# Turn-taking between VectorE and GpSimd in a fused GeGLU FFN (Strassen-Winograd) kernel

## The chip, the cores and the metric

One core of one Trainium2 chip. The metric is the device time of one launch in microseconds, median of several executions. In every execution here it is 1.7 to 1.9 us longer than the span of the profile (first to last instruction), and the granted TensorE clock was 0.998 to 1.000, so all runs are compared as fast ones. The runs came from several chips of the same kind; only kernels timed in the same rounds on the same chip are compared by ratio.

## The reference

```python
B, S, D, F = 1, 2048, 1024, 3584          # all bfloat16
def reference(x, w_gate, w_up, w_down):
    return (gelu_tanh(x @ w_gate) * (x @ w_up)) @ w_down
```

## The kernel before

The kernel computes each 2x2 block product with seven products in place of eight (Winograd's form). Sums of blocks of x (t1 to t4), of the gate and up weights (s1 to s4) and of w_down are made beside the matmuls. Rows are done in two halves (h = 0, 1); in each half the f tiles go in 14 pairs. In a pair TensorE does m1, m2 (of the pair before), m6, m5, m7, m3, m4, 8 matmuls each. Meanwhile GpSimd makes the 8 weight sums of the next pair, VectorE adds product m5 to banks in PSUM and multiplies by the gelu, and, in the first half only, VectorE makes 42 "staging" sums of w_down rows, into a pool of four buffers (o_sb) from which 28 of them are stored to DRAM for the later stage. A buffer of the same pool, the "x tile" below, is now and then filled with transposed x for the second half (DMA transposes) and stored to DRAM too. The parts that the change touches (cuts are marked):

```python
def pool(inst):
    if "pool_wait" in last_on:                       # a semaphore wait, once
        tc.add_manual_dep(inst.ins, last_on.pop("pool_wait").ins.name, SYNC_DEP, reason="port")
    return on("pool", inst)
def pool_behind_dve():
    last_on["pool_wait"] = last_on["dve"]
...                                                  # t_sum, for t4: all blocks on VectorE
    dve(tt(out=t[:, cs], in0=b(1, 0)[:, cs], in1=t2[:, cs], op=sub))
...                                                  # stage_step(n): one staging sum
    dve(nc.vector.tensor_tensor(out=t, in0=in0, in1=in1, op=ALU.subtract))
    if k > 0:
        sp(nc.sync.dma_start(out=t_dram[:, k - 1, i, :], in_=t.bitcast(F32)))
...                                                  # the loop over pairs, h == 0, pair >= 2
    n = [min(max(4 * (pair - PPG + d) - 2, 0), NSTEP) for d in range(3)]
    steps = [lambda k=k: stage_step(k) for k in range(n[0], n[1])]
    early_steps = steps[: len(steps) - 2]
    then["m2 of last"] = (load_chunk if any) + early_steps + (fill an x tile)
    then["m7"] = [load rows of w_down for the next pair] + [store_x]
    then["m4"] = steps[len(early_steps) :]           # two of them behind m4
```

So a pair's four staging sums stand in two places: two behind the last matmuls, in front of the next pair's product `out11` (the multiplication behind m2), two behind that. Nothing keeps them off GpSimd's sums.

Of the kernel before, what the change touches and what calls it, by code (L numbers as in the profile page):

```python
# [34 lines left out]
def kernel(  # L35
# [87 lines left out]
        return on("act", inst)  # L123

    def dve(inst):
        return on("dve", inst)

    def pool(inst):
        if "pool_wait" in last_on:

            tc.add_manual_dep(
                inst.ins, last_on.pop("pool_wait").ins.name, SYNC_DEP, reason="port"
            )
        return on("pool", inst)

    def pool_behind_dve():
        last_on["pool_wait"] = last_on["dve"]

    def pe(inst):
        return on("pe", inst)  # L140
# [86 lines left out]
    def t_sum(name, c0=0, c1=KH):  # L227
        def b(j, l):
            return xT[l][:, half(j), :]

        t0 = ("t1", "t2", "t3", "b22", "t4").index(name) * KH * TB
        t = t_mem[:, t0 : t0 + KH * TB].rearrange("p (a b) -> p a b", b=TB)
        tsum[name] = t
        sub = ALU.subtract
        tt = nc.vector.tensor_tensor
        if name == "t1":
            dve(tt(out=t, in0=b(0, 1), in1=b(0, 0), op=sub))
        elif name == "t2":
            t1 = tsum["t1"].bitcast(F32)
            dve(tt(out=t, in0=b(1, 1), in1=t1, op=sub))  # L240
        elif name == "t3":
            dve(tt(out=t, in0=b(1, 1), in1=b(0, 1), op=sub))
        elif name == "t4":
            t2 = tsum["t2"].bitcast(F32)
            cs = slice(c0, c1)
            dve(tt(out=t[:, cs], in0=b(1, 0)[:, cs], in1=t2[:, cs], op=sub))  # L246
        else:
            for c in range(KH):
                act(nc.scalar.copy(out=t[:, c, :], in_=b(1, 1)[:, c, :]))
# [126 lines left out]
    S_NAMES = ("s1", "s2", "s3", "s4", "a22")  # L376


    pending = []

    def pair_quads(hT, h, pair, nxt, then, part=None):
# [20 lines left out]
                f()  # L402

        def prep(j, name):
            if nxt is not None and part is None:
                s_sum(nxt[0], nxt[1], j, name)

        def s(j, name):
# [26 lines left out]
        def do_m5(j):  # L435
            mm(V_[j], j, s(j, "s1"), tsum["t1"], True)
            m5[j] = m_pool.tile([P, TB], F32, name=f"m5_{j}")
            act(nc.scalar.copy(out=m5[j][:], in_=banks[V_[j]][:]))  # L438
            prep(j, "s1")

        def do_m6(j):
            mm(QB[j], j, s(j, "s2"), tsum["t2"], False)
# [30 lines left out]
        for j in range(2):  # L473
            add_m5(QB[j], QB[j])
            done(f"q{j}")
            prep(j, "s2")
        done("m5")
        for j in range(2):
# [111 lines left out]


    staged = {}
    NSTEP = 3 * NS

    def stage_load(i):
        w = wd_pool.tile([P, WDT, D], BF16, name="wd_sb")
# [5 lines left out]
    def stage_step(n):  # L602
# [11 lines left out]
        if k > 0:  # L614
            sp(nc.sync.dma_start(out=t_dram[:, k - 1, i, :], in_=t.bitcast(F32)))



    staged_x = []

    def stage_x(tb, kd):
        if tb == 1:
            load_xT(xT, 1, tb, kd, kd + 1)
            return
        t = o_pool.tile([P, 1, TB], BF16, name="o_sb")
        src = xv[SH : SH + TB, kd : kd + 1, :]
        sp(nc.sync.dma_start_transpose(out=t[:], in_=src))
        staged_x.append((x_dram[:, kd : kd + 1, :], t[:]))

    def store_x():  # L630
        for dst, src in staged_x:
# [197 lines left out]
    for h in range(NH):  # L829
        hT = hT_pool.tile([P, KF, SH], BF16, name="hT")  # L830
        first_pair = 0
        if h == 0:
            first_units(hT)
            first_pair = PPG - 1

            nxt = (0, PPG)
            for j in range(2):
                s_sum(0, first_pair, j, "s3")
            pair_quads(hT, 0, first_pair, nxt, {}, 0)
            t_sum("t1")  # L840
            for j in range(2):
                s_sum(0, first_pair, j, "a22")
                for name in ("s1", "s2"):
                    s_sum(0, first_pair, j, name, True)
            for k0, k1 in ((0, KH // 2), (KH // 2, KH), (KH, KD)):
                for u, bset in enumerate((PB, RB)):
                    for b, w_sb in zip(bset, chunks[first]):
                        for kd in range(k0, k1):
                            mm_gu(banks[b], w_sb, u, 1, kd)
                    if k1 == KD:  # L850
                        unit_out(hT, bset, u, 1)
                    if k1 == KD and u == 0:
                        t_sum("t3")
                if k1 == KH:
                    out11 = pair_quads(hT, 0, first_pair, nxt, {}, 2)
                    t_sum("b22")
                    t_sum("t2")
                    s_sum(0, first_pair, 0, "s4", True)
            t_sum("t4", 0, KH // 2)
            s_sum(0, first_pair, 1, "s4", True)  # L860

            xs = [
                (tb, kd + i) for kd in range(0, KD, 2) for tb in (1, 0) for i in range(2)
            ]
            new_x(1)
            stage_load(0)
        for pair in range(first_pair, NPAIR):
            then = {}
            if pair % PPG == 0 and (pair // PPG + 1) * PPG < NPAIR:
                key = (h, pair // PPG + 1)  # L870

                def load_chunk(key=key):
                    new_chunk(key)
                    for j in range(2):
                        load_w(key, j, 0, KD, act)

                if key not in chunks:
                    then["m2 of last"] = [load_chunk]
            if h == 0 and pair >= PPG:

                n = [
                    min(max(4 * (pair - PPG + d) - 2, 0), NSTEP) for d in range(3)
                ]
                steps = [lambda k=k: stage_step(k) for k in range(n[0], n[1])]
                early_steps = steps[: len(steps) - 2]
                new = range((n[1] + 2) // 3, (n[2] + 2) // 3)

                then["m2 of last"] = (
                    then.get("m2 of last", [])
                    + early_steps  # L890
                    + [lambda q=q: stage_x(*q) for q in xs[:2]]
                )
                then["m7"] = [lambda i=i: stage_load(i) for i in new] + [store_x]
                then["m4"] = steps[len(early_steps) :]
                xs = xs[2:]
            if pair == NPAIR - 2:

                then.setdefault("m2 of last", []).extend(
# [1 line left out]
                )  # L900
            if 6 < pair < 11:
                i = 2 * pair - 8
                then.setdefault("m6", []).append(
                    lambda i=i: s_down(hT, 0, "s3", i, i + 2)
                )
            if pair == NPAIR - 1:
                then |= {
                    "m2 of last": [
                        lambda: load_b22(4, 10),
                        lambda: load_b22(10, NS),  # L910
                        lambda: early.append(
                            wd_pool.tile([P, WDT, D], BF16, name="wd_sb")
                        ),
                        lambda: s_down(hT, 0, "s3", 0, 4),
                    ],
                    "m6": [
                        lambda: s_down(hT, 0, "s1", 4, 8),
                        lambda: t_down(0, "t1", 4, 6),
                    ],
                    "m2": [  # L920
                        lambda: load_wd_rows(8, 10),
                        lambda: load_wd_rows(10, 12),
                        lambda: load_wd_rows(12, NS),
                        lambda: load_b22(0, 4),
                    ],
                    "m7": [lambda: s_down(hT, 0, "s1", 0, 4)],
                    "m3": [lambda: t_down(0, "t1", 0, 2)],
                    "m4": [
                        lambda: t_down(0, "t2", 0, NT2),
                        lambda: t_down(0, "t1", 2, 4),  # L930
                        lambda: t_down(0, "t1", 6, 8),
                        lambda: s_down(hT, 0, "s1", 8, NS),
                        lambda: t_down(0, "t1", 8, NS),
                    ],
                }
            if pair < PPG and h == 0:

                def late_t4(c):
                    t_sum("t4", c, c + 1)
                    last_on["t4"] = last_on["dve"]  # L940

                def late_s():
                    last_on["pool_wait"] = last_on["t4"]
                    for name in S_NAMES:
                        for j in range(2):
                            s_sum(0, PPG, j, name)

                then = {
                    "q0": [lambda: late_t4(KH - 2)],
                    "v0": [lambda: late_t4(KH - 1)],  # L950
                    "v1": [out11],
                    "m4": [late_s],
                }
# [6 lines left out]
        if h + 1 < NH:  # L960
# [1 line left out]
            new_x(0)  # L962

            def x_fill():
                sp(nc.sync.dma_start(out=xT[0][:], in_=x_dram[:]))

            def w_fill(c, j):
                if j == 0:
                    new_chunk((nh, c))
                n = 2 if c == 0 else 1  # L970
                for k0 in range(0, KD, KD // n):
                    load_w((nh, c), j, k0, k0 + KD // n)

            def s_fill(j, *names):
                for name in names:
# [58 lines left out]
```

## Time and profile before

| | before |
|---|---|
| median of the 3 executions known at the time (lowest to highest) | 541.09 us (540.6 to 542.26) |
| the execution that was profiled: time, span | 542.15 us, 540.4 us |
| TensorE / VectorE / GpSimd busy | 99% / 67% / 43% |
| period of a pair in either half | 12.56 us |
| stalls of TensorE for VectorE | 1.37 us in pair 3, 0.40 us in pair 1 |

The groups of instructions by shape on VectorE between 40 and 176 us, for the line of the staging sums (count, then busy us and mean ns of one):

```profile
L613 DVE TENSOR_TENSOR o_sb<-wd_sb,o_sb 128x512 fp32r<-128x512 bf16 x28 | 29.9, 1066 | 0.5
...
L613 DVE TENSOR_TENSOR o_sb<-wd_sb 128x512 fp32r<-128x512 bf16 x14 | 18.6, 1328 | 0.0
```

A sum that takes 0.68 us when it is free takes 1.07 and 1.33 us on average here.

### The profile page before, as it was taken

To read this page: it belongs to the slowest core of one execution; us is meant where nothing else is said; L and a number is where in the kernel's file an instruction comes from. 1 tells how busy PE (TensorE), PEld (TensorE's weight loads), DVE (VectorE), ACT (ScalarE), POOL (GpSimd) and SP (SyncE) were. 2 spreads that over 40 slices of the span, in tenths; PEclk is the share of its full clock that TensorE was granted. 3 is DMA by queue.
4 is the path that set the end of the run, shared out by engine and by line. 5 is a ranking of instruction groups with operands and counts; after the bars stand their busy time and mean duration, and the time that the engine had idled before them with its cause. 6 is when DMAs were issued, how large, how long until landed. Compare 5 with 4: busy or idle time off the path is not lost.

```text
span 540.4 us, 7111 instructions
## 1 busy us (share of the span) xinstructions
PE 534.3 (99%) x2384; PEld 377.4 (70%) x2384; DVE 363.9 (67%) x478; ACT 263.4 (49%) x446; POOL 233.8 (43%) x208
## 2 busy tenths in 40 slices
PE   9999999999999999999999999999999999999997
PEld 4576777767676676767776667777777766866865
DVE  1968777787877997889474334444444469969951
ACT  2554555555555319217465555555555551552270
POOL 1078777777777000000056776666777730000000
PEclk9999999999999999999999999999999999999999
DMA  9952877795726968689950505041231466677855
GB/s 224 281 175 85 258 215 231 213 285 177 252 98 222 354 223 310 199 279 300 323 184 1 156 1 157 13 144 61 95 112 45 156 207 219 226 233 244 284 158 202
DMA packets 84372, 102.70 MB, mean 190 GB/s; under 512 B 18672, under 2 KB 66288, under 8 KB 84208
## 3 DMA queue, kind: packets, MB, share of 16 engines
q1 hardware_dynamic: 61936, 80.49, 46.1%
q10 hardware_dynamic: 22400, 21.76, 13.0%
q8 instruction: 19, 0.31, 0.2%
q14 instruction: 17, 0.14, 0.1%
HBM read 85.98 MB, written 12.58 MB: 182 GB/s over the span
## 4 chain that ended last, share of the span: by engine, by line
PE 97%; DVE 1%; DMA 1%; ACT 0%; issue 0%; ACTq 0%
PE bank L390 62%; PE bank L678 33%; PE bank L254 3%; DVE o_sb L613 1%; DMA w_mem<-in_x_dram 1%; PE bank L305 0%; DVE hT L278 0%; ACT s_mem L374 0%; ACT o_sb L731 0%; ACT w_mem L273 0%; DVE xT L313 0%; ACTq L731 0%; ACTq L374 0%
## 5 line engine op out<-in xcount | busy, mean ns | idle before, releaser
L390 PE MATMUL bank<-t_mem,s_mem 128*128 128x512 f32 x1056 | 250.0, 395 | 1.1 <-DVE hT L278 1.1
L390 PEld LDWEIGHTS bank<-t_mem,s_mem 128*128 128x128 f32 x1056 | 198.1, 188 | 45.7 <-DVE hT L278 1.5
L361 POOL TENSOR_TENSOR s_mem<-w_mem 128x512 fp32r<-128x512 bf16 x102 | 117.2, 1171 | 202.7 <-DVE t_mem L246 103.0
L678 PE MATMUL bank<-t_mem,s_mem 128*128 128x512 f32 x544 | 127.1, 392 | 0.0
L278 DVE TENSOR_TENSOR hT<-w_mem,bank 128x512 bf16<-128x512 f32 x104 | 71.0, 686 | 82.9 <-PE bank L390 42.9
L678 PEld LDWEIGHTS bank<-t_mem,s_mem 128*128 128x128 f32 x544 | 102.2, 188 | 22.1
L413 DVE TENSOR_TENSOR bank<-bank,m 128x512 f32<-128x512 f32 x108 | 69.9, 694 | 47.2 <-ACT m L438 43.9
L390 PE MATMUL bank<-xT,w_mem 128*128 128x512 bf16 x432 | 98.1, 380 | 0.0
L273 ACT ACTIVATE w_mem<-bank 128x512 f32<-128x512 f32 x104 | 61.8, 596 | 54.1 <-DVE bank L413 35.7
L390 PEld LDWEIGHTS <-w_mem 128*128 128x128 bf16 x432 | 40.2, 98 | 51.7 <-issue 6.8
L588 DVE TENSOR_TENSOR t_mem<-w_mem 128x1024 fp32r<-128x1024 bf16 x56 | 65.6, 1218 | 0.0
L361 POOL TENSOR_TENSOR s_mem<-w_mem,s_mem 128x512 fp32r<-128x512 bf16 x50 | 61.7, 1260 | 0.0
L361 POOL TENSOR_TENSOR s_mem<-s_mem,w_mem 128x512 fp32r<-128x512 f32 x50 | 57.6, 1173 | 0.0
L443 ACT COPY bank<-bank 128x512 f32<-128x512 f32 x54 | 30.8, 570 | 39.0 <-PE bank L390 38.5
L374 ACT CAST s_mem<-w_mem 128x512 fp32r<-128x512 bf16 x54 | 33.1, 616 | 31.9 <-PE bank L390 29.2
L438 ACT COPY m<-bank 128x512 f32<-128x512 f32 x54 | 31.7, 587 | 19.7 <-PE bank L390 19.2
L653 DVE TENSOR_TENSOR s_mem<-hT 128x512 fp32r<-128x512 bf16 x52 | 34.2, 686 | 10.1 <-PE bank L678 9.4
L678 PEld LDWEIGHTS <-hT 128*128 128x128 bf16 x224 | 21.3, 98 | 26.6 <-issue 2.1
L448 ACT COPY bank<-bank 128x512 f32<-128x512 f32 x54 | 30.7, 570 | 12.1 <-PE bank L390 12.1
L731 ACT CAST o_sb<-bank 128x512 bf16<-128x512 f32 x28 | 15.6, 586 | 39.2 <-PE bank L678 33.5
L613 DVE TENSOR_TENSOR o_sb<-wd_sb,o_sb 128x512 fp32r<-128x512 bf16 x28 | 29.9, 1066 | 0.5
L585 ACT CAST t_mem<-w_mem 128x1024 fp32r<-128x1024 bf16 x28 | 26.9, 1048 | 0.0
(45 smaller groups left out, 239.9 us busy)
## 6 DMA issues: line engine op xcount, KB each, us to landing
t_mem<-t_dram SPq DMA_DIRECT2D x56, 512.0 KB, 5.1
w_mem<-in_w_gate_dram ACTq DMA_DIRECT2D x10, 1024.0 KB, 5.7
w_mem<-in_w_up_dram ACTq DMA_DIRECT2D x10, 1024.0 KB, 7.9
wd_sb<-in_w_down_dram SPq DMA_DIRECT2D x28, 256.0 KB, 4.7
t_dram<-o_sb SPq DMA_DIRECT2D x28, 256.0 KB, 2.4
wd_sb<-in_w_down_dram SPq DMA_DIRECT2D x12, 512.0 KB, 4.6
w_mem<-in_w_down_dram SPq DMA_DIRECT2D x10, 512.0 KB, 6.9
w_mem<-in_w_down_dram SPq DMA_DIRECT2D x4, 1024.0 KB, 6.3
```

The source lines that it names most:

```text
L273: act(nc.scalar.activation(out=g_sb, in_=ps[:], func=ACT.Gelu_apprx_tanh))
L278: nc.vector.tensor_tensor(out=hT[:, fc, tb * TB : (tb + 1) * TB], in0=g_sb, in1=ps[:], op=ALU.mult,)
L361: pool(nc.gpsimd.tensor_tensor(out=t, in0=in0, in1=in1, op=op))
L374: act(nc.scalar.copy(out=t, in_=a(1, 1)))
L390: nc.tensor.matmul(banks[bank][:], lhsT=lhs[:, c, :], rhs=rhs[:, c, :], start=start and c == 0, stop=c == KH - 1, skip_group_check=True,)
L413: nc.vector.tensor_tensor(out=banks[dst][:], in0=banks[src][:], in1=m5[j][:], op=ALU.add)
L438: act(nc.scalar.copy(out=m5[j][:], in_=banks[V_[j]][:]))
L443: act(nc.scalar.copy(out=banks[RB[j]][:], in_=banks[QB[j]][:]))
L588: dve(nc.vector.tensor_tensor(out=t, in0=in0, in1=in1, op=ALU.subtract))
L613: dve(nc.vector.tensor_tensor(out=t, in0=in0, in1=in1, op=ALU.subtract))
L653: dve(nc.vector.tensor_tensor(out=t, in0=in0, in1=in1, op=op))
L678: nc.tensor.matmul(banks[bset[u]][:], lhsT=lhs(i, u), rhs=rhs(i), start=start and i == 0, stop=stop and i == NS - 1, skip_group_check=True,)
```

## The change

Its intent: VectorE and GpSimd take turns in SBUF. In each pair of the first half VectorE does all its staging sums in one run, behind GpSimd's last sum, and GpSimd starts its next sums behind the run. To fit, one of GpSimd's eight sums (s4 of the up weights) moves into VectorE's run, and two blocks of t4, which stood between PSUM additions in pair 1, go to GpSimd. The core of the diff (shortened; load_chunk and x tile stand for longer expressions):

```diff
     def dve(inst):
+        if "dve_wait" in last_on:
+            tc.add_manual_dep(inst.ins, last_on.pop("dve_wait").ins.name, SYNC_DEP, reason="port")
         return on("dve", inst)
+    def dve_behind_pool():
+        last_on["dve_wait"] = last_on["pool"]
@@ t_sum, t4
-            dve(tt(out=t[:, cs], ...))
+            if c0 > 0:
+                tt = nc.gpsimd.tensor_tensor
+            (pool if c0 > 0 else dve)(tt(out=t[:, cs], ...))
+    N_STEPS = [0, 0, 0, 4, 5, 5, 5, 4, 4, 4, 4, 4, 3, 0]
@@ prep
+            on_dve = (j, name) == (1, "s4") and in_turns(h, pair + 1)
@@ loop over pairs
-                then["m2 of last"] = load_chunk + early_steps + x tile
-                then["m4"] = steps[len(early_steps) :]
+                in_turn = [lambda k=k: stage_step(k) for k in interleaved(n[0], n[1])]
+            if in_turns(h, pair):
+                in_turn.insert(1, lambda pair=pair: s_sum(0, pair, 1, "s4", True))
+            if in_turn:
+                in_turn = [dve_behind_pool] + in_turn + [pool_behind_dve]
+            then["m2 of last"] = load_chunk + in_turn + stage_xs
```

(Cut: t4 blocks 2 and 3 are made behind the last DVE sum in front of pair 1; the x tile takes two transposes in place of one; later loads of x and weights are split in halves; GpSimd makes the s1 sums behind the first PSUM addition and not before it; the sums of hT of pairs 7 to 10 join VectorE's run; staging sums are reordered so that one seldom stands right behind the one that it reads, and the first weight rows are loaded later.)

More of the change, by code (lines that the diff above doesn't have):

```diff
@@ L125, in dve @@
     def dve(inst):
+        if "dve_wait" in last_on:
+            tc.add_manual_dep(
+                inst.ins, last_on.pop("dve_wait").ins.name, SYNC_DEP, reason="port"
+            )
         return on("dve", inst)
@@ L245, in t_sum @@
             cs = slice(c0, c1)
-            dve(tt(out=t[:, cs], in0=b(1, 0)[:, cs], in1=t2[:, cs], op=sub))
+            if c0 > 0:
+                tt = nc.gpsimd.tensor_tensor
+            (pool if c0 > 0 else dve)(
+                tt(out=t[:, cs], in0=b(1, 0)[:, cs], in1=t2[:, cs], op=sub)
+            )
         else:
@@ L376, with in_turns @@
     S_NAMES = ("s1", "s2", "s3", "s4", "a22")
+    N_STEPS = [0, 0, 0, 4, 5, 5, 5, 4, 4, 4, 4, 4, 3, 0]
+    assert len(N_STEPS) == NPAIR
+    def in_turns(h, pair):
+        return h == 0 and pair < NPAIR and N_STEPS[pair] > 0
     pending = []
@@ L404, in prep @@
         def prep(j, name):
-            if nxt is not None and part is None:
+            on_dve = (j, name) == (1, "s4") and in_turns(h, pair + 1)
+            if nxt is not None and part is None and not on_dve:
                 s_sum(nxt[0], nxt[1], j, name)
@@ L438, in do_m5 @@
             act(nc.scalar.copy(out=m5[j][:], in_=banks[V_[j]][:]))
-            prep(j, "s1")
         def do_m6(j):
@@ L475, in pair_quads @@
             done(f"q{j}")
+            if j == 0:
+                prep(0, "s1")
+                prep(1, "s1")
             prep(j, "s2")
@@ L592 @@
     staged = {}
-    NSTEP = 3 * NS
+    assert sum(N_STEPS) == 3 * NS
     def stage_load(i):
@@ L615, in stage_step, with interleaved @@
             sp(nc.sync.dma_start(out=t_dram[:, k - 1, i, :], in_=t.bitcast(F32)))
+    def interleaved(n0, n1):
+        left, order = list(range(n0, n1)), []
+        while left:
+            done = {-1, *range(n0), *order}
+            free = [k for k in left if k % 3 == 0 or k - 1 in done]
+            apart = [k for k in free if k % 3 == 0 or k - 1 not in order[-1:]]
+            order.append((apart or free)[0])
+            left.remove(order[-1])
+        return order
     staged_x = []
@@ L622, in stage_x @@
         if tb == 1:
-            load_xT(xT, 1, tb, kd, kd + 1)
+            for k in (kd, kd + 1):
+                load_xT(xT, 1, tb, k, k + 1)
             return
-        t = o_pool.tile([P, 1, TB], BF16, name="o_sb")
-        src = xv[SH : SH + TB, kd : kd + 1, :]
-        sp(nc.sync.dma_start_transpose(out=t[:], in_=src))
-        staged_x.append((x_dram[:, kd : kd + 1, :], t[:]))
+        t = o_pool.tile([P, 2, TB], BF16, name="o_sb")
+        for k in range(2):
+            src = xv[SH : SH + TB, kd + k : kd + k + 1, :]
+            sp(nc.sync.dma_start_transpose(out=t[:, k : k + 1, :], in_=src))
+        staged_x.append((x_dram[:, kd : kd + 2, :], t[:]))
     def store_x():
@@ L860 @@
             s_sum(0, first_pair, 1, "s4", True)
-            xs = [
-                (tb, kd + i) for kd in range(0, KD, 2) for tb in (1, 0) for i in range(2)
-            ]
+            pool_behind_dve()
+            for c in range(KH // 2, KH):
+                t_sum("t4", c, c + 1)
+            xs = [(tb, kd) for kd in range(0, KD, 2) for tb in (1, 0)]
             new_x(1)
-            stage_load(0)
         for pair in range(first_pair, NPAIR):
@@ L878 @@
                     then["m2 of last"] = [load_chunk]
+            in_turn, stage_xs = [], []
             if h == 0 and pair >= PPG:
-                n = [
-                    min(max(4 * (pair - PPG + d) - 2, 0), NSTEP) for d in range(3)
-                ]
-                steps = [lambda k=k: stage_step(k) for k in range(n[0], n[1])]
-                early_steps = steps[: len(steps) - 2]
-                new = range((n[1] + 2) // 3, (n[2] + 2) // 3)
-                then["m2 of last"] = (
-                    then.get("m2 of last", [])
-                    + early_steps
-                    + [lambda q=q: stage_x(*q) for q in xs[:2]]
-                )
+                n = [sum(N_STEPS[:q]) for q in (pair, pair + 1, pair + 2)]
+                in_turn = [lambda k=k: stage_step(k) for k in interleaved(n[0], n[1])]
+                new = range((n[1] + 2) // 3, (n[2] + 2) // 3)
+                stage_xs = [lambda q=q: stage_x(*q) for q in xs[:1]]
                 then["m7"] = [lambda i=i: stage_load(i) for i in new] + [store_x]
-                then["m4"] = steps[len(early_steps) :]
-                xs = xs[2:]
+                xs = xs[1:]
             if pair == NPAIR - 2:
@@ L902 @@
                 i = 2 * pair - 8
-                then.setdefault("m6", []).append(
-                    lambda i=i: s_down(hT, 0, "s3", i, i + 2)
-                )
+                in_turn.append(lambda i=i: s_down(hT, 0, "s3", i, i + 2))
+            if in_turns(h, pair):
+                in_turn.insert(1, lambda pair=pair: s_sum(0, pair, 1, "s4", True))
+            if in_turn:
+                in_turn = [dve_behind_pool] + in_turn + [pool_behind_dve]
+            then["m2 of last"] = then.get("m2 of last", []) + in_turn + stage_xs
             if pair == NPAIR - 1:
@@ L913 @@
                         ),
+                        dve_behind_pool,
                         lambda: s_down(hT, 0, "s3", 0, 4),
@@ L936 @@
             if pair < PPG and h == 0:
-                def late_t4(c):
-                    t_sum("t4", c, c + 1)
-                    last_on["t4"] = last_on["dve"]
                 def late_s():
-                    last_on["pool_wait"] = last_on["t4"]
                     for name in S_NAMES:
@@ L948 @@
                 then = {
-                    "q0": [lambda: late_t4(KH - 2)],
-                    "v0": [lambda: late_t4(KH - 1)],
                     "v1": [out11],
@@ L964, in x_fill @@
             def x_fill():
-                sp(nc.sync.dma_start(out=xT[0][:], in_=x_dram[:]))
+                for k0 in range(0, KD, KH):
+                    src = x_dram[:, k0 : k0 + KH, :]
+                    sp(nc.sync.dma_start(out=xT[0][:, k0 : k0 + KH, :], in_=src))
             def w_fill(c, j):
@@ L969, in w_fill @@
                     new_chunk((nh, c))
-                n = 2 if c == 0 else 1
-                for k0 in range(0, KD, KD // n):
-                    load_w((nh, c), j, k0, k0 + KD // n)
+                for k0 in range(0, KD, KH):
+                    load_w((nh, c), j, k0, k0 + KH)
             def s_fill(j, *names):
```

## The prediction

> **What bounds the kernel now.** I read the page first (busy shares and the chain that ended last), then TensorE's waits, then timelines of TensorE, VectorE and GpSimd for two kinds of f-tile pair. The page of the kernel before:
>
> ```profile
> PE 534.3 (99%) x2384; PEld 377.4 (70%) x2384; DVE 363.9 (67%) x478; ACT 263.4 (49%) x446; POOL 233.8 (43%) x208
> ...
> PE 97%; DVE 1%; DMA 1%; ACT 0%; issue 0%; ACTq 0%
> ```
>
> TensorE is the chain from end to end. A busy matmul row is not yet a matmul at full rate, so I took the pace as well: how far apart do the pairs start? TensorE's timeline in the first half of the rows, where the weight differences are staged (VectorE and GpSimd both work in SBUF):
>
> ```profile
> 95.13 3.63 PE L390 MATMUL bank<-xT,w_mem 128*128 128x512 bf16 x16
> 98.41 9.44 PE L390 MATMUL bank<-t_mem,s_mem 128*128 128x512 f32 x40
> 107.69 3.63 PE L390 MATMUL bank<-xT,w_mem 128*128 128x512 bf16 x16
> ```
>
> and in the second half, where VectorE stages nothing:
>
> ```profile
> 296.06 3.63 PE L390 MATMUL bank<-xT,w_mem 128*128 128x512 bf16 x16
> 299.34 9.44 PE L390 MATMUL bank<-t_mem,s_mem 128*128 128x512 f32 x40
> 308.62 3.63 PE L390 MATMUL bank<-xT,w_mem 128*128 128x512 bf16 x16
> ```
>
> Both periods are 12.56 us (107.69 - 95.13 and 308.62 - 296.06), for 56 matmuls: 224 ns each. So in the regular pairs the contention between VectorE and GpSimd costs the end nothing. What TensorE and its weight loads lose to other engines is in the list of waits:
>
> ```profile
> PE bank L390 <- DVE hT L278: 1.1, 1, 1.1
> ...
> PEld bank L390 <- DVE hT L278: 1.5, 1, 1.5
> ...
> PEld bank L390 <- DVE bank L413: 0.7, 2, 0.4
> ```
>
> One stall and two small ones, no more. The large one is in pair 3 (starts at 43.49). VectorE there:
>
> ```profile
> 44.59 5.00 DVE L613 TENSOR_TENSOR o_sb<-wd_sb 128x512 fp32r<-128x512 bf16 x1
> 49.62 0.69 DVE L613 TENSOR_TENSOR o_sb<-wd_sb,o_sb 128x512 fp32r<-128x512 bf16 x1
> 50.23 0.68 DVE L278 TENSOR_TENSOR hT<-w_mem,bank 128x512 bf16<-128x512 f32 x1
> ```
>
> A staging sum that takes 0.69 us when free took 5.00 us, until GpSimd's run of 16 sums back to back (31.04 to 49.04) had ended. Behind it stood the product that frees a PSUM bank, so TensorE stood until 50.97. From starts of single matmuls in the trace: the gap was 1.49 us and the next 0.34, where 0.227 each is normal. Loss: 1.49 + 0.34 - 2 x 0.227 = 1.37 us. The two small ones, in pair 1, have gaps of 0.34, and of 0.40 and 0.34: losses 0.11 and 0.29 us.
>
> **What the Trainium skill says.** "SBUF — State Buffer", section "Who interferes with whom": a VectorE instruction with two SBUF inputs contends with a GpSimd instruction that reads SBUF, one with at most one SBUF input does not, and the loser blocks fully. The trace agrees: 5.00 against 0.69 us for the staging sum, while L413 and L278 (one input in PSUM) stay at 0.69 under GpSimd's work. "GPSIMD Engine Reference", section "3.1 Elementwise — side-by-side cycle accounting", gives 1.96 times VectorE's time for an add of two inputs; here GpSimd's start-to-start spacing is about 1.13 us (two in 2.29) and VectorE's 0.61 (28.42, 29.02), 1.85 times. "Perfetto Trace Analysis", section "Identifying the Most-Contended Engine", warns against matmul busy share as a measure of headroom; I therefore argue from the 12.56 us period.
>
> **The change, part by part.** TensorE's 2384 matmuls and ScalarE's instructions stay the same.
>
> (a) Turns. In pairs 3 to 12 of the first half, VectorE does its 3 to 5 staging sums in one run, behind GpSimd's last sum for the pair; GpSimd starts the next sums behind the run. In the kernel before, the 42 staging sums take 48.5 us (29.9 for 28 of them with an o_sb input, 18.6 for the other 14: mean 1.15); at 0.69 they take 29, some 20 us less VectorE time. All but pair 3 of it lies beside TensorE. In pair 3 nothing stands in front of the product any more: 1.37 us gained, if GpSimd is done in time. It now begins when its two T4 blocks end, 27.9 + 2 x 1.13 + about 0.05 = 30.2, and has 15 sums before the turn: 30.2 + 15 x 1.13 = 47.15. VectorE gets to its turn at about 43.2 + 4.46 = 47.7. No wait.
>
> (b) T4 blocks 2 and 3 to GpSimd. They stood between the PSUM additions of pair 1 (VectorE at 28.42 and 30.22). Without the first, the second addition starts at 28.42 rather than 29.02 and ends at 29.1, ahead of the weight load that waits for it (29.37). The 0.29 us loss goes; the 0.11 stays, since the sum in front of that addition stays. GpSimd has the blocks by 30.25, their matmuls come after 30.7.
>
> (c) One weight sum (s4 of the second matrix) to VectorE in ten pairs: GpSimd falls from 8 sums to 7 in a pair, 7 x 1.13 = 7.9 us; VectorE gains 0.61 in its run.
>
> (d) Transposes in pairs, x and weights filled in halves: transfers, with nobody on TensorE waiting for them.
>
> **What the turns cost.** Take the start of a pair's first bf16 matmul as zero, from the pair at 95.13. The product ahead of the turn starts at 98.99, +3.86; the next VectorE instruction can start at 99.59, +4.46. The first PSUM addition must be over before the first weight load of m3, which starts in the trace at 103.84, +8.71; 0.11 us of lateness is caught up there (the 0.24 late load of pair 1 cost 0.13 at most). Now that addition starts at +7.03 (it waits for ScalarE). In the changed kernel it comes behind the whole run:
> - 5 instructions in the run (pairs 3 and 11; 4 in pair 12): +4.46 + 5 x 0.61 = +7.51, ends at +8.21. In time.
> - 6 in the run (pairs 4 to 10: five staging sums and s4, or four, s4 and one sum of hT): +4.46 + 6 x 0.61 = +8.12, plus 0.70 for the addition and 0.05 to TensorE: +8.87. Late by 0.16, of which 0.11 is caught up: 0.05 lost. Where a sum comes right behind the one that it reads (spacing 0.71 at 99.59 to 100.30), 0.1 more. The built order of VectorE has such neighbours: one in pairs 4, 6 and 9, two in pair 8, none in 5, 7 and 10.
> Sum: 7 x 0.05 + 5 x 0.1 = 0.85 us lost. Later additions have slack: the second ends at +9.5 against +9.6, those of m7 at +10.1 against +10.5.
>
> The turn itself must also close: the run ends at +8.2, GpSimd's 7 sums last 7.9, so it is done at +16.15, which is +3.6 of the next pair, and VectorE asks at +4.46. Slack 0.85 us in each pair, and TensorE needs the earliest of these sums (s2) only at +15.6, done at +11.7.
>
> **Sum.** 1.37 + 0.29 - 0.85 = 0.8 us gained: 541.09 - 0.8 = 540.3 us. In words: a large cut in VectorE's time, off the critical path, and a net change of some 0.15%.
>
> **Rivals.**
> 1. The run is short enough everywhere (VectorE's spacing nearer to 0.60, additions not held): nothing is lost in m3, and the gain is the whole 1.66: 539.4. For it: 0.60 is seen too (28.42 to 29.02). Against: two DMA waits stand ahead of some sums in the run, and can only add.
> 2. The waits move onto TensorE: each turn costs two semaphore hops, and a late transfer (the 2.4 us stores that free an o_sb buffer, or a weight row) holds the run and with it four additions. At 0.5 us more in each of ten pairs: +5, 545.3. For it: the slack in m3 is gone in seven pairs. Against: buffers that a run fills were stored in the pair before, 8 us earlier, and weight rows are asked for in m7, some 7 us ahead, against 4.7 to landing.
> 3. The contention costs TensorE something in each pair that the profile hides, and its removal speeds all of them up. Against: the equal 12.56 us with and without staging. Even 0.2 us in ten pairs would be 2 us, 538.
> 4. GpSimd's turn does not close and the loop of VectorE and GpSimd becomes the period: 4.4 + 7.9 + hops = 12.5 against 12.56. It would take 0.9 us of extra delay in a pair to reach TensorE; then a few tenths a pair, 542 to 544.
>
> **Range and chances.** Timed runs of before spread from 540.6 to 542.26, so noise is about as large as the effect. Rival 1 sets the lower side, a mild rival 2 or 4 the upper: 538.9 to 541.6. A gain over 2% would need 10.8 us, more than all TensorE waits on other engines together; a loss over 2% would need 1 us in each turn. Chances: faster 0.005, same 0.98, slower 0.015.
>
> **What would show it.** Right: staging sums at a mean near 0.69 us, VectorE some 15 us less busy, no stall near 51 us, the product wait of 1.1 us gone from TensorE's list, and in its place weight loads in pairs 4 to 10 waiting some 0.1 to 0.3 us for the PSUM addition; pair periods of 12.56 in the second half and 12.6 to 12.8 in the first. Wrong: staging sums still over 1 us (the turns do not keep the engines apart), VectorE waiting for GpSimd in every turn (the loop binds), or a first-half period below 12.56.

## The result, and the profile after

Changed kernel: 541.79 us (541.33 to 542.38, 6 executions); before, in the same rounds: 541.44 us (540.6 to 542.26, 6). Ratio 1.0006, 95% interval 0.9993 to 1.0019: the same. A ratio here is the mean time of one kernel's fast runs over that of the other's of the same rounds, so it is not quite the ratio of the medians quoted. The predicted 540.3 and its range up to 541.6 were missed by 0.2 us at the upper end. The profiled execution, though, had a span of 539.5 us against 540.4: 0.9 us less, about what was predicted. Two facts that do not fit together; the experiments are about that.

The page of the changed kernel:

```profile
PE 532.4 (99%) x2348; PEld 377.1 (70%) x2384; DVE 347.7 (64%) x486; ACT 263.3 (49%) x446; POOL 219.5 (41%) x200
...
PE 98%; DMA 1%; issue 0%; ACT 0%; DVE 0%; ACTq 0%
```

VectorE is 16.2 us less busy (363.9 - 347.7); the matmul count is lower only because 36 records are missing. The groups of staging sums, same stretch as above (the line is now L634):

```profile
L634 DVE TENSOR_TENSOR o_sb<-wd_sb,o_sb 128x512 fp32r<-128x512 bf16 x28 | 18.8, 687 | 0.3
L634 DVE TENSOR_TENSOR o_sb<-wd_sb 128x512 fp32r<-128x512 bf16 x14 | 9.5, 684 | 0.0
```

The turns keep the two engines apart: 0.69 and 0.68 us. TensorE's waits hold no other engine's sums any more:

```profile
PE bank L208 <- PEq L1044: 0.8, 1, 0.8
PE bank L265 <- DVE xT L324: 0.2, 1, 0.2
PE bank L316 <- DMA w_mem<-in_x_dram: 0.2, 1, 0.2
```

What came in its place stands in the waits of the weight loads, four times, under the name "issue" (the view names no releaser; that it is the PSUM addition is read from the times below, and in the run "dose" the matmuls' waits name it):

```profile
PEld bank L408 <- issue: 1.0, 4, 0.3
```

Pair 8 shows it. VectorE's timeline there: the product, the run of six, the additions:

```profile
109.77 0.69 DVE L289 TENSOR_TENSOR hT<-w_mem,bank 128x512 bf16<-128x512 f32 x1 [2.61 <-PE bank L408]
110.38 0.68 DVE L634 TENSOR_TENSOR o_sb<-wd_sb,o_sb 128x512 fp32r<-128x512 bf16 x1
110.98 0.69 DVE L370 TENSOR_TENSOR s_mem<-w_mem,s_mem 128x512 fp32r<-128x512 bf16 x1
111.58 0.68 DVE L634 TENSOR_TENSOR o_sb<-wd_sb 128x512 fp32r<-128x512 bf16 x1
112.30 1.42 DVE L634 TENSOR_TENSOR o_sb<-wd_sb,o_sb 128x512 fp32r<-128x512 bf16 x2
113.63 0.68 DVE L688 TENSOR_TENSOR s_mem<-hT 128x512 fp32r<-128x512 bf16 x1
114.24 2.48 DVE L432 TENSOR_TENSOR bank<-bank,m 128x512 f32<-128x512 f32 x4
```

The first addition starts at 114.24 and lasts 0.69 us, to 114.93. By the trace of single instructions, m3's first weight load follows at 115.04, and the gaps of the two matmuls are 0.334 and 0.306 us where 0.227 each is normal. Pair 8 is the longest of all at 12.79 us.

### The profile page after: what moved, and what is told of

Read it like the earlier page. It is cut to its first block, busy times and chain, and to the rows that moved or that the text cites. A ratio compares the mean times of both kernels' runs of the same rounds, so it can differ in the third digit from the quotient of the medians.

```text
span 539.5 us, 7070 instructions
## 1 busy us (share of the span) xinstructions
PE 532.4 (99%) x2348; PEld 377.1 (70%) x2384; DVE 347.7 (64%) x486; ACT 263.3 (49%) x446; POOL 219.5 (41%) x200
## 4 chain that ended last, share of the span: by engine, by line
PE 98%; DMA 1%; issue 0%; ACT 0%; DVE 0%; ACTq 0%
PE bank L408 63%; PE bank L713 33%; PE bank L265 3%; DMA w_mem<-in_x_dram 1%; PE bank L316 0%; ACT o_sb L766 0%; ACT bank L466 0%; DVE xT L324 0%; ACTq L766 0%; ACTq L466 0%
## 5 line engine op out<-in xcount | busy, mean ns | idle before, releaser
L408 PE MATMUL bank<-xT,w_mem 128*128 128x512 bf16 x406 | 96.7, 380 | 1.4
L372 POOL TENSOR_TENSOR s_mem<-w_mem,s_mem 128x512 fp32r<-128x512 bf16 x40 | 45.9, 1162 | 0.0
L713 PE MATMUL bank<-w_mem,hT 128*128 128x512 bf16 x108 | 24.7, 379 | 0.2
```

What stands on the lines that cost most here:

```text
L372: pool(nc.gpsimd.tensor_tensor(out=t, in0=in0, in1=in1, op=op))
L408: nc.tensor.matmul(banks[bank][:], lhsT=lhs[:, c, :], rhs=rhs[:, c, :], start=start and c == 0, stop=c == KH - 1, skip_group_check=True,)
L713: nc.tensor.matmul(banks[bset[u]][:], lhsT=lhs(i, u), rhs=rhs(i), start=start and i == 0, stop=stop and i == NS - 1, skip_group_check=True,)
```

## Where a profile puts its time

Since the pace of a pair is exact, losses can be read off one profile after the other: the start of the first f32 matmul of a pair, less that of the pair before, less 12.56 us. This table holds all profiles but that of "dose"; "pair 1" is the stretch from the first to the second such start; "tail" is from the start of the last matmul to the end of the span.

| profile | pair 1 | lost in pair 3 | lost in 4, 5, 6, 7, 8, 9, 10 | sum of 4 to 10 | tail | span |
|---|---|---|---|---|---|---|
| before | 11.32 | 1.39 | none | 0.00 | 4.18 | 540.4 |
| before_1 | 11.05 | 0.00 | none | 0.00 | 4.53 | 539.5 |
| before_2 | 10.88 | 1.40 | none | 0.00 | 4.27 | 540.3 |
| before_3 | 10.87 | 1.33 | none | 0.00 | 4.37 | 540.8 |
| before_4 | 10.85 | 1.35 | none | 0.00 | 4.55 | 541.3 |
| after | 10.86 | 0.00 | .06 .03 .11 .00 .23 .09 .03 | 0.54 | 4.48 | 539.5 |
| after_1 | 10.85 | 0.00 | .11 .03 **1.51** .03 .23 .07 .00 | 1.97 | 4.32 | 540.7 |
| after_2 | 10.91 | 0.00 | .11 .00 **1.46** .03 .19 .10 .03 | 1.91 | 4.55 | 541.0 |
| after_3 | 10.86 | 0.00 | .09 .01 .10 .03 .23 .09 .00 | 0.55 | 4.65 | 539.7 |
| no_s4 | 10.83 | 0.00 | none | 0.00 | 3.86 | 538.8 |
| no_s4_2 | 10.85 | 0.00 | none | 0.00 | 3.87 | 538.9 |
| no_s4_x | 10.88 | 0.00 | none | 0.00 | 3.67 | 538.3 |
| x_early | 11.05 | 0.00 | .07 .00 .06 .01 .23 .06 .03 | 0.46 | 3.69 | 539.4 |
| store_first | 10.85 | 0.00 | .07 .19 **1.73** .03 .19 .24 .03 | 2.49 | 4.61 | 542.3 |
| no_s4_sf | 11.00 | 0.00 | .00 .45 **1.82** .00 .00 .00 .00 | 2.27 | 3.86 | 540.6 |
| t4_only | 10.84 | 1.67 | none | 0.00 | 4.36 | 540.7 |
| late_start | 11.03 | 1.89 | none | 0.00 | 4.42 | 541.5 |

The start of the first f32 matmul lies anywhere from 22.83 to 23.61 us, and the stretch behind pair 10 varies by up to 0.7 us, in all kernels; that is noise of the first loads and of later transfers which no experiment here touches.

## The experiments

Sixteen kernels ran. Theory A: what the profile of before showed in pair 3 is a race that comes in some executions and not in others, and the changed kernel has a chance stall of its own. Theory B: the block comes always, and the change gives its gain back elsewhere. All gave correct results.

### The kernel before again: before_1 and before_2

No edit but a comment.

> The kernel before, once more, for its profile and for the span of each timed execution. Theory A (the 5.00 us block of pair 3 is chance: VectorE and GpSimd race for SBUF, and in some executions VectorE gets in between two GpSimd sums): spans vary between about 538.8 and 540.5 us, the profile shows a gap in pair 3 of another size than 1.37 us, perhaps none. Theory B (the block comes in every execution, and the change gives back elsewhere what it gains): the same 1.37 us loss in pair 3 in this profile too, spans near 540.0.

> A second profile of the kernel before. Theory A: the loss in pair 3 differs from that of the other profiles (0 to 1.4 us). Theory B: 1.37 us again.

Measured: before_2, one execution, 542.07 us. before_1 541.3 us (540.91 to 542.59, 5 executions) against 542.29 of the same kernel in the same rounds: ratio 0.9989, interval 0.9976 to 1.0003. That is a kernel against itself, and shows how much one may read into 0.1%. The profile of before_1 has no stall in pair 3. VectorE there:

```profile
44.77 1.64 DVE L613 TENSOR_TENSOR o_sb<-wd_sb 128x512 fp32r<-128x512 bf16 x1
46.44 1.53 DVE L613 TENSOR_TENSOR o_sb<-wd_sb,o_sb 128x512 fp32r<-128x512 bf16 x1
47.89 0.67 DVE L278 TENSOR_TENSOR hT<-w_mem,bank 128x512 bf16<-128x512 f32 x1
```

and GpSimd beside it:

```profile
44.70 2.72 POOL L361 TENSOR_TENSOR s_mem<-w_mem 128x512 fp32r<-128x512 bf16 x2
47.38 3.20 POOL L361 TENSOR_TENSOR s_mem<-w_mem,s_mem 128x512 fp32r<-128x512 bf16 x2
```

The same sum that took 5.00 us in the first profile took 1.64: VectorE got in between two of GpSimd's sums, which then took 1.6 us in place of 1.17, and the product came 2.3 us earlier, in time. In before_2 it was 4.96 us again and 1.40 us were lost. Theory A holds for the block.

### The changed kernel again: after_1, after_2

> The changed kernel once more. Both theories: no loss in pair 3, 0.4 to 0.6 us lost in pairs 4 to 10 at the start of m3, in the same pairs as in the first profile (turns leave nothing to chance on VectorE). Theory A: its mean span equals that of before within 0.5 us, while before's spread is larger.

> The changed kernel, third profile. In the last profile of it VectorE stood 1.3 us inside the run of pair 6, for the store of the x tile whose o_sb buffer the run takes over. Theory: that is chance of the transfer (a late landing of the store); so here 0 or some 1 us in pair 6, and 0.4 to 0.6 us in m3 of the pairs with 6 instructions either way.

Measured: after_1 542.63 us (542.54 to 542.94, 5) against 542.29, ratio 1.0008, interval 0.9996 to 1.0021; after_2 542.63 (541.88 to 542.79, 4) against 542.32, ratio 1.0002, interval 0.9978 to 1.0026. The expectation that turns leave nothing to chance was wrong. The losses in m3 come back to within 0.06 us in the same pairs, but pair 6 has 1.5 us that the first profile did not have. VectorE in after_1's pair 6:

```profile
86.34 0.69 DVE L634 TENSOR_TENSOR o_sb<-wd_sb 128x512 fp32r<-128x512 bf16 x1
88.34 0.69 DVE L634 TENSOR_TENSOR o_sb<-wd_sb 128x512 fp32r<-128x512 bf16 x1 [1.32 <-DMA x_dram<-o_sb]
```

In the middle of the run it waits for a store: the fourth instruction writes an o_sb buffer that held the x tile of pair 5. The queue of pair 5 in after_1:

```profile
75.07 1.52 SPq L636 DMA_DIRECT2D t_dram<-o_sb  x3
76.64 3.69 SPq L662 DMA_TRANSPOSE o_sb<-in_x_dram  x2
80.38 2.01 SPq L620 DMA_DIRECT2D wd_sb<-in_w_down_dram  x4
82.50 0.37 SPq L667 DMA_DIRECT2D x_dram<-o_sb  x1
```

Stores of the run, transposes that fill the tile, loads of weight rows, and only then the tile's own store, which VectorE had to wait for until 88.3. In the first profile of the changed kernel the store was issued at 81.91, and VectorE found the buffer free. The transposes (2.46 us of the queue there) are not the whole difference: in after_2, which stalled too, they took 2.47 us, the loads 2.92, and the store was issued at 82.30. The landings in the traces say more. Without the stall the store landed at 86.56 and 86.61 (after, after_3), some 0.35 us before VectorE asked for the buffer; with it at 88.32 and 88.37 (after_1, after_2). Issued 0.4 to 0.7 us later, it landed 1.7 to 1.8 us later: it also took 5.8 and 6.1 us from issue to landing in place of 4.7 and 4.8 (2.4 to 2.9 for the three other x tiles of each of these profiles). Why the landing varies is open.

### One superfluous sum in each run: dose

```diff
+                if 4 <= pair <= 10:
+                    in_turn.insert(3, lambda pair=pair: s_sum(0, pair, 1, "s4", True))
```

> The changed kernel with one superfluous sum (s4 once more, same result) in each run of pairs 4 to 10. If a run's length goes straight to TensorE through the first addition of m3: 0.61 us more in each of seven pairs, 4.0 us in sum (some repeats fall between two dependent sums and hide 0.1), 545.5 to 546. If TensorE has slack that the profile hides: under 2 us.

Measured: 545.72 us (545.49 to 546.13, 4) against 542.32, ratio 1.0063, interval 1.0034 to 1.0091. Its profile loses .71 .57 .71 .55 .71 .69 .55 in pairs 4 to 10, 4.47 us in sum against 0.54 in the first profile after: 3.9 more, 4.0 expected. TensorE's waits now name the addition in all seven pairs, and the weight loads wait seven times, under "issue" again:

```profile
PE bank L408 <- DVE bank L432: 2.6, 7, 0.4
```

```profile
PEld bank L408 <- issue: 5.4, 7, 0.8
```

So beyond six instructions a run's length goes almost whole to TensorE through the first PSUM addition. (This kernel had no stall in pair 6: the store landed at 87.86, and the buffer was asked for at 88.74; without the repeat in that run it would have been 88.1, still behind the landing.)

### One sum less in each run: no_s4, no_s4_2

```diff
-            on_dve = (j, name) == (1, "s4") and in_turns(h, pair + 1)
+            on_dve = False
-            if in_turns(h, pair):
-                in_turn.insert(1, lambda pair=pair: s_sum(0, pair, 1, "s4", True))
```

> The changed kernel with the s4 sum left on GpSimd: runs of 5 at most on VectorE, 8 sums on GpSimd. If the runs' length is what TensorE waits for in m3: no waits in pairs 4 to 10, 0.5 us less than the changed kernel (some 541.2 us). GpSimd should be done at +16.65, which is +4.09 of the next pair, ahead of VectorE at +4.46. Rival: the turn no longer closes, VectorE waits for GpSimd at each turn and the pairs of the first half grow over 12.56 us: 541.8 or more.

> no_s4 once more, on another chip. If its 0.31% gain was the kernel: again 0.2 to 0.35% under before, no losses in m3. If the store of the x tile came in time by luck: a stall in pair 6 in this profile, smaller by 0.5 us than in the changed kernel, and 0.1% or less gained.

Measured: no_s4 540.62 us (539.91 to 540.8, 5) against 542.29, ratio 0.9969, interval 0.9956 to 0.9981; no_s4_2 on another chip 540.51 (540.2 to 541.16, 6) against 541.69, ratio 0.9973, interval 0.9947 to 0.9999. Neither profile loses anything in pairs 3 to 10. With eight sums left on GpSimd the turn still closes: VectorE waited for GpSimd once in each profile, 0.4 and 0.6 us, at the first turn, and TensorE did not notice. The move of s4 was thus not needed and cost the 0.5 us in m3. No pair 6 stall showed in either profile; the store landed 0.6 and 0.7 us before it was needed. The five and six timed executions lie within 0.9 and 1.0 us, less than the stall's 1.4, so it was hardly among them either; that it cannot come is not shown. Against after_1 in the same rounds (542.63 us) no_s4 is 2.0 us faster, more than the 0.5 expected: after_1's profile has 1.4 us of stall besides.

### Issuing the tile's store ahead of the loads: store_first, no_s4_sf

```diff
-                then["m7"] = [lambda i=i: stage_load(i) for i in new] + [store_x]
+                then["m7"] = [store_x] + [lambda i=i: stage_load(i) for i in new]
```

> The changed kernel with one edit: in m7 the x tile's store is issued ahead of the weight rows' loads, some 2 us earlier. If the stall in pair 6 comes from that store standing behind the loads in the queue: no wait of VectorE for it in any pair, the m3 losses unchanged at 0.4 to 0.6 us, time like the changed kernel's executions without the stall (541.3) and less spread. Rival: the store waits for the transposes themselves, and the loads now come late: waits for weight rows in the runs.

> Both edits: s4 left on GpSimd and the store ahead of the loads. Runs of 5 have 0.5 us more slack in m3, so no losses there, and no wait for the store: the pairs of the first half at 12.56 us, 0.2 to 0.4% faster than the kernel before, like no_s4 alone where the store came in time.

Measured: store_first 542.33 us (541.74 to 544.04, 6) against 542.32, ratio 1.0002, interval 0.9981 to 1.0024; no_s4_sf 542.66 (541.24 to 543.32, 6), ratio 1.0001, interval 0.9979 to 1.0022. The rival was right. (The profiled execution of store_first, 544.04 us, was the slowest of its six.) The wait for the store is gone and one for the weight rows stands in its place, in pair 6 again. VectorE's waits in store_first between 30 and 176 us:

```profile
DVE o_sb L634 <- DMA wd_sb<-in_w_down_dram: 1.5, 1, 1.5
```

The queue then stands until the transposes have landed, and the loads behind it come late; no_s4_sf lost 1.82 us in pair 6 the same way, slack or no slack. (Its VectorE waited for GpSimd in three turns, 1.3 us in all; the 0.45 us lost in pair 5 stand beside waits for weight rows of 0.34 and 0.55 us.)

### Filling the tile earlier: x_early, no_s4_x

```diff
-            then["m2 of last"] = then.get("m2 of last", []) + in_turn + stage_xs
+            then["m2 of last"] = then.get("m2 of last", []) + stage_xs + in_turn
```

> The changed kernel with one edit: the transposes that fill the x tile are issued ahead of the run's stores instead of behind them, so the tile is filled, stored and free earlier and VectorE's run in pair 6 finds its buffer free. If that store is what stops the run: no wait of VectorE for a transfer in pair 6, m3 losses unchanged at 0.4 to 0.6 us, 1 us less than the changed kernel where it had the stall (542.6 on the last two chips): 541.3 to 541.6. Rival: the queue as a whole is late there (as with the store ahead of the loads, where the wait moved to the weight rows): a wait of 1 us or more in pair 6 under another name.

> Both: s4 left on GpSimd, x tile filled early. All pairs of the first half at 12.56 us; profile as no_s4's best one, 538.8 us span; 540.6 us, about 0.2 to 0.3% under the kernel before.

Measured: x_early 541.22 us (540.54 to 541.56, 6) against 541.69, ratio 0.9983, interval 0.9959 to 1.0008: no wait for a transfer in any of VectorE's runs, m3 losses as before at 0.46 us. The tile's store is issued some 3 us earlier:

```profile
78.92 0.43 SPq L667 DMA_DIRECT2D x_dram<-o_sb  x1
```

It landed at 84.23, and at 84.31 in no_s4_x, 3.0 and 2.2 us before the buffer was asked for. no_s4_x, with both edits, 540.17 us (539.75 to 540.37, 6), ratio 0.9966, interval 0.9942 to 0.999. This is the fastest version, and its executions lie within 0.6 us (before on that chip: 540.61 to 544.2). Its TensorE timeline, at pair 8:

```profile
106.07 3.63 PE L408 MATMUL bank<-xT,w_mem 128*128 128x512 bf16 x16
109.35 9.44 PE L408 MATMUL bank<-t_mem,s_mem 128*128 128x512 f32 x40
118.63 3.63 PE L408 MATMUL bank<-xT,w_mem 128*128 128x512 bf16 x16
```

12.56 us, like every pair from 3 on. Not all of the gain is turns: the tail in the five profiles without the move of s4 or with the early tile (no_s4, no_s4_2, no_s4_sf, no_s4_x, x_early) is 3.67 to 3.87 us against 4.18 to 4.65 in all others. The difference lies in the landing of the last output store (1.70 us from issue to landing in no_s4_x, 2.26 in before, 2.49 in after), which no edit touched; why it differs by build is open. Some 0.6 us of the 1.5 are that.

### Part (b) alone: t4_only

The kernel before with only t4's blocks 2 and 3 moved to GpSimd (the lines of the diff under "t_sum, t4", and GpSimd's sums no longer wait for the last t4 block on VectorE).

> The kernel before with part (b) alone: T4 blocks 2 and 3 on GpSimd, no turns. Pair 1 should lose 0.3 to 0.45 us less (second half of the run 0.4 earlier up to pair 3). GpSimd's 16 sums start 0.8 us earlier; if the 5 us block of pair 3 happens, it lasts to their end at about 48.2, and the loss there is 0.6 to 0.9 us instead of 1.37; if VectorE gets in between, none.

Measured: 542.9 us (542.46 to 544.98, 6) against 541.69, ratio 1.0022, interval 0.9995 to 1.0048. Pair 1 took 10.84 us. The expectation for pair 3 was too low: 1.67 us lost.

```profile
44.22 4.20 DVE L617 TENSOR_TENSOR o_sb<-wd_sb 128x512 fp32r<-128x512 bf16 x1
...
49.66 1.62 DVE L617 TENSOR_TENSOR o_sb<-wd_sb,o_sb 128x512 fp32r<-128x512 bf16 x1
51.20 1.65 DVE L617 TENSOR_TENSOR o_sb<-wd_sb 128x512 fp32r<-128x512 bf16 x1
52.78 2.48 DVE L417 TENSOR_TENSOR bank<-bank,m 128x512 f32<-128x512 f32 x4
```

The block did get shorter, 4.20 us. But GpSimd began its next sums sooner, too, met the next two staging sums (1.62, 1.65) and through them delayed the additions: a second stall of TensorE, at m3.

### The block taken out of the product's way: late_start

```diff
                 early_steps = steps[: len(steps) - 2]
+                if pair == PPG:
+                    held_back, steps = steps, []
+                elif pair == PPG + 1:
+                    early_steps = held_back + early_steps
+                    steps = held_back + steps
```

> The kernel before with one edit: the first two staging sums come behind the product of pair 3 and not in front of it, so a block by GpSimd's last sums holds only sums that have slack. No turns, s4 and T4 as before. If the block in front of that product is what makes before's executions spread: no stall in pair 3, VectorE held until about 49.0 at most and the first addition at about 51.0 to 51.7, ahead of m3 at 52.2; no execution over 541.6, median 541.0. If executions over 542 stay, other pairs have blocks of their own.

Measured: 543.07 us (542.63 to 543.65, 6) against 542.01, ratio 1.002, interval 0.9994 to 1.0047. My expectation failed. The product is now in time, but the four staging sums behind it are held in turn:

```profile
48.26 1.76 DVE L613 TENSOR_TENSOR o_sb<-wd_sb 128x512 fp32r<-128x512 bf16 x1
50.05 2.27 DVE L613 TENSOR_TENSOR o_sb<-wd_sb,o_sb 128x512 fp32r<-128x512 bf16 x2
52.24 1.64 DVE L613 TENSOR_TENSOR o_sb<-wd_sb 128x512 fp32r<-128x512 bf16 x1
53.80 2.48 DVE L413 TENSOR_TENSOR bank<-bank,m 128x512 f32<-128x512 f32 x4
```

The addition comes at 53.80, 2.1 us behind the latest start that was expected (51.7), and TensorE lost 1.89 us at m3. Moving the sums only moves the collision; with the turns it is gone in all eleven profiles that have them. Which of the two waits does it, VectorE's for GpSimd's last sum or GpSimd's for the run's end, was not tested apart.

### How often: before_3, before_4, after_3

> A fourth profile of the kernel before. Either the block of pair 3 (VectorE some 5 us in one sum, 1.2 to 1.4 us lost on TensorE, span over 540.2) or none (under 539.6). A span over 541 would be one of the slow executions (some of before's were at 543 to 544.2 us) and shows what else can block.

> A fifth profile of the kernel before, with the same two outcomes: a block in front of pair 3's product and a span over 540.2 us, or none and a span under 539.6 us.

> A fourth profile of the changed kernel: m3 losses of 0.4 to 0.6 us in pairs 4 to 10 again; in pair 6 VectorE's wait for the x tile's store either near 0 (span 539.5) or 1.3 us (span 540.7 to 541.1).

Measured: before_3 542.54 us and before_4 543.12 us, one execution each, both with the block (4.92 and 4.94 us; 1.33 and 1.35 us lost). after_3: 542.68 us (541.12 to 543.6, 6) against 542.01, ratio 1.0014, interval 0.9984 to 1.0043; its profiled execution (541.47 us) had no stall in pair 6, three others of it took 543.26 us and more. The block came in 4 of 5 profiles of before, the stall in pair 6 in 2 of 4 profiles of the changed kernel. The timed executions suggest other shares, and that they differ from chip to chip: the six of before beside the result form two groups, 540.6 to 541.09 and 541.8 to 542.26, while on chip 14 all nine were at 541.94 to 542.57 and all five of after_1 at 542.54 to 542.94. Without a profile each this is not shown. Executions of before at 544 us were not caught in a profile and stay unexplained.

## Why the prediction was wrong, step by step

**The starting point.** The step that failed first is "541.09 - 0.8 = 540.3 us": a gain read from one profile was taken off a median of other executions. That profile was of an execution 1 us slower than the median, and 1.37 of the 1.37 + 0.29 = 1.66 us of gross gain, the "1.37 us gained" of part (a), is a race which that execution had lost. The size in such an execution was right (0 against 1.33 to 1.40). The mean over five profiles of before is (1.39 + 0 + 1.40 + 1.33 + 1.35) / 5 = 1.09 us. Taken off the profiled execution itself, 0.8 us gives 542.15 - 0.8 = 541.35; the profiled execution of the changed kernel took 541.33. That it fits so well is partly luck: m3 cost 0.3 us less than worked out, and the tail was 0.3 us longer.

**Part (b), 0.29 us.** Right in mechanism, too large as a term, for the same reason: pair 1 took 11.32 us in the profile that I read and 10.85 to 11.05 in the other four. What differs is how late VectorE is there. The sum in front of the additions started 4.34 us behind pair 1's first f32 matmul in that profile, and 0.11 + 0.29 us were lost; in before_2 to before_4 it started at 3.80 to 3.85, and nothing was lost. no_s4_sf, which has part (b), was as late (4.33) and lost 0.11 alone. Means 10.99 before and 10.87 after: 0.12 us.

**What the turns cost, 0.85 us.** Mechanism right, down to the pairs: most in pair 8, where I counted two dependent neighbours, nearly nothing in 5, 7 and 10. Size 0.54 and 0.55 in the two profiles without a stall: pairs 4, 6 and 9 lost 0.06 to 0.11 where 0.15 was worked out. "dose" confirms the slope, 0.56 us for each further instruction (3.9 / 7). Rival 1 (nothing lost in m3) is refuted by the 0.54.

**Rival 2, dismissed.** This is the second step that failed. "Buffers that a run fills were stored in the pair before, 8 us earlier" is wrong for one buffer: the x tile's, whose store was issued 4.4 to 5.1 us before the run asked for it, behind transposes and four loads in the queue. And "the 2.4 us stores" was the median of the staging sums' stores in the kernel before; in the changed kernel it is 5.4. The stall that the x tile brings, about 1.4 us in 2 of 4 profiles, is what the prediction lacks. Rival 4 (the turn does not close) did not come, not even with eight sums on GpSimd, apart from the short waits above. Rival 3 (a hidden cost in every pair) is refuted: before loses 0.00 us in pairs 4 to 10 in five profiles. The signs that the prediction named as right came (staging sums at 0.69 us, VectorE 16.2 us less busy, no stall in pair 3, pairs of up to 12.79 us), but none of them looks at the baseline or at the x tile.

**The sum with measured terms.** Gain 1.09 + 0.12, loss (0.54 + 1.97 + 1.91 + 0.55) / 4 = 1.24: 0.03 us slower. The four ratios were 1.0006, 1.0008, 1.0002 and 1.0014. The large cut in VectorE's time is where the prediction put it, off the critical path. Against the predicted gain of 0.8 us, the smaller gain takes 0.45, the stall of pair 6 0.69 on average, and m3 gives 0.30 back. The race, the stall and the cost in m3 are each shown; that their averages cancel fits the profiles, but five and four profiles fix such frequencies only roughly.

**What the change was good for.** Its turns do take the race away: 0.00 us in pair 3 in all eleven profiles with turns, dose included. What spoiled it were two details: the move of s4 and the place of the x tile's transposes (no_s4 alone showed no stall either, so how much the second is worth without the first is open). Without both it is 0.34% faster than before, of which some 0.6 us (0.1%) is the tail that no edit explains. A fifth o_sb buffer, which would have freed the run of the store another way, does not fit: the build refuses it (10 KB per partition wanted, 9.59 KB left).

## What to carry to other kernels

Before taking the gain of a stall off a median, look whether the profiled execution is a typical one: a second profile of the same kernel costs little and here would have cut the forecast gain. Where two engines collide by chance, moving one instruction moved the collision here; a wait at both ends of a short run removed it, and then each instruction in the run, each buffer that it takes over and the queue order of that buffer's store are on the clock. Count the slack up to the first consumer, and keep the run under it rather than at it.

## What the Trainium skill lacked or had wrong

- "SBUF — State Buffer", section "Who interferes with whom", says that issue order decides who blocks, for the whole instruction of the other. It does not say who is next when both queue: in 4 of 5 profiles a VectorE sum with two SBUF inputs was passed over by GpSimd sums that started after it until GpSimd paused (4.92 to 5.00 us, with GpSimd's spacing at 1.13 us), in one it got in at the next gap (1.64 us), and then GpSimd's sums stretched to 1.6 us.
- "GPSIMD Engine Reference", section "3.1 Elementwise — side-by-side cycle accounting", gives 1.96 for the ratio of the two engines at 2048 fp32 elements, and none for a smaller size; at 512 elements (mostly bf16 inputs) the spacing from start to start here is 1.13 against 0.61 us, 1.85.
- No page that I read has how lateness of a weight load turns into lost time: 0.11 us of it was caught up in the trace of the kernel before, and past that each further VectorE instruction of 0.61 us cost 0.56 us.
